# Row-wise exponentials on ScalarE in place of a subtraction and a row sum on VectorE, in linear attention with two MoE layers behind it

## The chip, the cores and the metric

The kernel runs on one core of a Trainium2 chip. The metric is the time of one execution on the device in microseconds, 1206.53 us as the median of three runs before the change. Five engines work side by side, each in its own program order: TensorE (PE for matmuls, PEld for weight loads), VectorE (DVE), ScalarE (ACT), GpSimd (POOL) and SyncE (SP, which issues the DMAs).

## The reference, cut to what matters

```python
# q, k, v: (8, 8, 576, 64)   batch, heads, tokens, head width
q_s = exp(q - max(q, -1));  q_s = q_s / (sum(q_s, -1) + 1e-9)   # along the 64 of a head
k_s = exp(k - max(k, 2));   k_s = k_s / (sum(k_s, 2) + 1e-9)    # along the tokens
out = q_s @ (k_s^T @ v)                                         # per head, 64 x 64 in between
x   = out as (4608, 512)
# first MoE layer: each token goes to argmax(x @ w_gate), one of 8 experts
x   = gate * sigmoid gate * (relu(x @ w1[e]) @ w2[e])
# second layer: the maximum of three products, then one more product
out = max(x @ W1, x @ W2, x @ W3) @ w_out
```

The change concerns only `q_s`: the maximum, the exponential and the sum over the 64 numbers of each head and token.

## The kernel before, in words

The kernel has two long parts. In the first, which lasts until about 600 us, attention and the first MoE layer are interleaved; the second MoE layer follows. The change touches the first part.

The first part is written as a list of slots. `moe_slot(slot)` issues one group of the MoE layer (`l1_group` or `l2_group`, 12 matmuls of 128 x 288 with a PSUM evacuation) and then the events that `at(slot, f, ...)` put into that slot. A batch has 32 slots: eight groups of the first product, eight of the second, for each of two halves of the hidden width. The schedule is manual: each engine runs its instructions in the order in which the slots issue them.

Attention comes in 16 units, one for each batch and half of the heads (`b, hb = divmod(n, 2)`), each spread over slots relative to its start `START[n] = 16 n - 51`, so a unit starts every 16 slots. `STEADY` gives the offsets of the first ten steps (`FRONT`): q_max -4, q_exp -1, k_max -4, k_tr 0, k_exp 1, q_sum 3, kv_mm 6, kv_norm 6, kv_lo 7, q_norm 8. Then come, for both pairs of heads (`BACK`), q_tr 10 and 15, q_lo 10 and 16, x_mm 13 and 17, x_lo 14 and 18, logit_mm 15 and 19. Units 0 to 3 have slots of their own. As a unit starts 16 slots after the one before it, slots -4 to 3 of a unit are slots 12 to 19 of the one before: the second half of its BACK steps and the FRONT steps of the next unit share slots. Events of the earlier unit come first in a slot.

A q tile has 128 partitions and 20 rows of 64 numbers (4 heads, 5 pieces of tokens). `q_max` (L230) takes the maximum of the 20 rows on VectorE. `q_exp` subtracts it (L237, VectorE; on GpSimd for one unit) and takes the exponential of all 1280 numbers in one ScalarE instruction (L238). `q_sum` sums the 20 rows on VectorE (L268), adds 1e-9 and takes the reciprocal (L269, L270). `q_norm` (L277) multiplies.

The other steps that the prediction names: `k_tr` transposes the key maxima (kT, L245), reduces them (L247) and forms the diagonal tiles dg with two products (L250); `k_exp` spreads them over the partitions with a matmul (kB, L257), subtracts on VectorE (L260) and takes the exponential on ScalarE (ke, L262). `q_tr` transposes q on TensorE and copies the upper part on ScalarE (qTs, L336), `q_lo` forms the lower part on VectorE (L344), and `x_mm` (xT, L362) multiplies with both, so it waits for q_lo. `logit_mm` (L390) copies the logits on ScalarE after the last pair (lgt, L393 and L394); one slot later `logit_tr` transposes them on TensorE (lg, L399), `route_1` follows on VectorE, and `route_2` counts with a matmul (cnt, L425).

Each MoE group is evacuated from one of four PSUM banks (`ps_mm`, bufs=4): in `l1_group` by a relu on ScalarE (L625) and a difference on VectorE (L626); in `l2_group` by a copy on ScalarE (L643) for the first half of the hidden width, and by an addition on VectorE (L645) for the second. The even units' slots -2 to 2 fall on groups with the ScalarE copy, those of the odd units on groups with the VectorE addition. Expert weights are split on ScalarE (L597) and GpSimd (L604), the weights of the second layer are decoded in three steps that share VectorE, ScalarE and GpSimd (L687 to L706), and the routing table is written by indirect DMAs from GpSimd (L498).

Of the kernel before, what the change touches and what calls it, by code (L numbers as in the profile page):

```python
# [9 lines left out]
F32 = mybir.dt.float32  # L10
# [3 lines left out]
ACTF = mybir.ActivationFunctionType  # L14
ALU = mybir.AluOpType
AX = mybir.AxisListType
# [37 lines left out]
ROUTE = (20, 22)  # L54
ROUTE0 = (7, 9)
ROUTE1 = (17, 19)
DEC = ((5, 10), (3, 8, 11), (18, 26))


@with_exitstack  # L60
def tile_linear_attention__then__moe(
# [18 lines left out]
    vec = nc.vector  # L80
    act = nc.scalar.activation
# [48 lines left out]
    sm = es_att.enter_context(tc.tile_pool(name="sm", bufs=2, side="right"))  # L130
# [52 lines left out]
    units = {}  # L183
# [35 lines left out]
    def k_max(b, hb):  # L219
        u = units[b, hb]  # L220
        u["mx"] = sm.tile([128, 4, D], F32, tag="kmx", name="kmx")
        vec.tensor_reduce(
            out=u["mx"], in_=u["k"].rearrange("p h c d -> p h d c"), axis=AX.X, op=ALU.max
        )

    def q_max(b, hb):
        u = units[b, hb]
        qt = u["q"].rearrange("p h c d -> p (h c) d")
        m = sm.tile([128, 20, 1], F32, tag="qm", name="qm")
        vec.tensor_reduce(out=m[:, :, 0], in_=qt, axis=AX.X, op=ALU.max)  # L230
        u["qm"] = m
# [274 lines left out]
    def at(slot, f, *args):  # L506
        events.setdefault(slot, []).append((f, args))
# [4 lines left out]
    def in_2(b, f):  # L512
        f(1, 0)

    first = (
        (load_k, 0), (load_k, 1), (load_q, 0), (load_v, 0), (load_q, 1), (load_v, 1),
        (k_max, 0), (k_tr, 0), (k_max, 1), (k_exp, 0), (k_tr, 1), (q_max, 0), (k_exp, 1), (q_exp, 0),
        (kv_mm, 0), (q_max, 1), (q_sum, 0), (kv_mm, 1), (q_norm, 0), (q_exp, 1), (kv_norm, 0), (q_tr, 0, 0), (kv_lo, 0),
        (load_2,), (q_sum, 1), (q_lo, 0, 0), (q_tr, 0, 1), (x_mm, 0, 0), (kv_norm, 1), (q_lo, 0, 1), (kv_lo, 1),
        (q_norm, 1), (q_tr, 1, 0), (x_mm, 0, 1), (logit_mm, 0, 0), (q_tr, 1, 1), (x_mm, 1, 0), (logit_mm, 0, 1),  # L520
        (x_mm, 1, 1), (x_lo, 0, 0), (x_lo, 0, 1), (logit_mm, 1, 0), (logit_mm, 1, 1), (in_2, q_max), (in_2, k_max),
        (logit_tr,), (route_1,), (route_2,), (in_2, q_exp), (x_lo, 1, 0), (x_lo, 1, 1), (route_3,),
    )
# [3 lines left out]
    for c in range(5):  # L527
        at(ROUTE0[1] + 2 * c, route_5, 0, c)
    START = {n: 16 * n - 51 for n in range(2, 2 * B)}
    FRONT = (q_max, q_exp, k_max, k_tr, k_exp, q_sum, kv_mm, kv_norm, kv_lo, q_norm)  # L530
    BACK = (q_tr, q_lo, x_mm, x_lo, logit_mm)
    for n, s0 in START.items():
        b, hb = divmod(n, 2)
        if n in EARLY:
            t, s0 = EARLY[n], 0
        else:
            t = STEADY
        if n > 2:
            at(LOAD.get(n, START.get(n - 2, 0) + 9), load_unit, b, hb)
        for d, f in zip(t[0], FRONT):  # L540
            if d is not None:
                at(s0 + d, f, b, hb)
        for pr in range(2):
            for d, f in zip(t[1 + pr], BACK):
                at(s0 + d, f, b, hb, pr)
        if hb == 1:
            s0 = START[n]
            r1, r2 = (s0 + ROUTE[0], s0 + ROUTE[1]) if n > 3 else ROUTE1
            at(r1, logit_tr, b)
            at(r1, route_1, b)  # L550
            at(r2, route_2, b)
            at(r2 + 3, route_3, b)
            at(r2 + 4, route_4, b)
            for c in range(5):
                at(r2 + 5 + 2 * c, route_5, b, c)
# [151 lines left out]

    dslots = [START[n] + o for n in range(4, 2 * B) for o in DEC[n % 2]] + [START[2 * B - 1] + o for o in DEC[2]]
    assert len(dslots) == 32
# [169 lines left out]
    with tc.manual_schedule():  # L879
# [458 lines left out]
        for c in range(6):  # L1338
# [41 lines left out]
            for i, (col, x) in enumerate(tiles):  # L1380
                m = CAP if x is None else 128
# [20 lines left out]
    with tc.For_i(0, n_trip, 1) as it:  # L1402
# [32 lines left out]
        for f in range(6):  # L1435
# [15 lines left out]
            h = lp.tile([128, 2, SLOT], F32R, tag=f"lh{f}", name="lh")  # L1451
# [44 lines left out]
```

## Time and profile before

| | |
|---|---|
| median of 3 runs | 1206.53 us (1205.19 to 1210.18) |
| profiled execution | 1209.64 us, its span 1207.9 us |
| PE busy | 1146.5 us, 95% of the span |
| DVE busy | 799.1 us, 66% |
| ACT busy | 527.4 us, 44% |
| POOL busy | 411.2 us, 34% |
| mean granted TensorE clock | 0.98 |

The page shows one execution. Busy time says how long an engine worked, not whether anybody waited for it; the waits and the timelines say that. A timeline row has the start, the duration (of all instructions that it merges), the engine, the line, the operation, the tiles written and read, the shapes and the count, and in brackets the idle time before it with what ended it.

### The profile page before, as it was taken

The page shows a single profiled execution, that of the slowest core. Times are in us where ns is not written, and L with a number is a line of the kernel's source. Part 1 is how long each engine was busy: PE and PEld are TensorE (multiplying, and loading weights), DVE is VectorE, ACT ScalarE, POOL GpSimd, SP SyncE. Part 2 cuts the span into 40 slices and gives each one's busy share as a digit, 9 for nine tenths or more (in the row PEclk, how much of TensorE's full clock was granted, in tenths as well). Part 3 has the DMA queues.
Part 4 walks back from the last instruction along what each step waited for, and adds up shares of the span by engine and source line. Part 5 has one row for each costly group of instructions (what it writes and reads, how often), then busy time and mean ns, then how long its engine had stood idle before and what let it go on. Part 6 is the DMA issues. An engine that isn't in the chain of part 4 may idle for free. (4 is left out here: it accounts for less than half of the span.)

```text
span 1207.9 us, 21422 instructions
## 1 busy us (share of the span) xinstructions
PE 1146.5 (95%) x7626; PEld 1072.1 (89%) x7626; DVE 799.1 (66%) x1500; ACT 527.4 (44%) x1081; POOL 411.2 (34%) x502
## 2 busy tenths in 40 slices
PE   4699999999989999999999999999999999999994
PEld 3599898989989898999999899899899989989983
DVE  7688788787878879655789565555546545564430
ACT  2454454635545453545455433443344244333220
POOL 1156667677666767768342030000000000000000
PEclk9899899999999999999999999999999999999997
DMA  6785557575645764436599588397768848747701
GB/s 162 181 224 135 160 170 218 153 208 156 180 159 170 203 177 137 137 115 204 195 311 311 176 256 285 134 296 242 235 217 272 270 144 286 242 149 221 225 26 41
DMA packets 204207, 234.95 MB, mean 195 GB/s; under 512 B 78253, under 2 KB 122061, under 8 KB 204096
## 3 DMA queue, kind: packets, MB, share of 16 engines
q1 hardware_dynamic: 202384, 233.14, 62.4%
q8 instruction: 62, 1.02, 0.3%
q0 software_dynamic: 1712, 0.39, 0.2%
q14 instruction: 49, 0.40, 0.1%
HBM read 189.56 MB, written 44.13 MB: 193 GB/s over the span
## 5 line engine op out<-in xcount | busy, mean ns | idle before, releaser
L638 PE MATMUL yp<-h,w 128*128 128x288 f32 x1536 | 227.0, 304 | 0.0
L620 PE MATMUL hp<-xs,w 128*128 128x288 f32 x1536 | 218.6, 299 | 0.0
L638 PEld LDWEIGHTS yp<-h,w 128*128 128x128 f32 x1536 | 213.1, 192 | 3.3
L620 PEld LDWEIGHTS hp<-xs,w 128*128 128x128 f32 x1536 | 208.2, 189 | 2.6
L604 POOL TENSOR_TENSOR w<-stg,w 128x512 fp32r<-128x512 f32 x126 | 181.2, 1441 | 68.5 <-ACT w L597 66.7
L1218 PE MATMUL pY<-t,sw 128*128 128x384 f32 (+1 forms) x972 | 193.5, 342 | 1.3 <-ACT s L1227 0.9
L1218 PEld LDWEIGHTS pY<-t,sw 128*128 128x128 f32 x972 | 172.8, 188 | 5.5 <-ACT s L1227 2.1
L1195 POOL DMA_INDIRECT out_dram<-ocx,ftb x1 | 1.0, 981 | 481.7 <-SPq L1402 481.7
L1306 PE MATMUL op<-wo,hc 128*128 128x512 f32 (+1 forms) x666 | 156.2, 394 | 0.0
L1306 PEld LDWEIGHTS op<-wo,hc 128*128 128x128 f32 (+1 forms) x666 | 125.1, 188 | 27.9
L1227 ACT ACTIVATE s<-pY 128x384 f32<-128x384 f32 (+1 forms) x108 | 53.7, 497 | 133.1 <-PE pY L1218 129.2
L626 DVE SCALAR_TENSOR_TENSOR h<-hp,h 128x288 fp32r<-128x288 f32 x128 | 56.6, 451 | 54.8 <-ACT h L625 54.4
L625 ACT ACTIVATE h<-hp 128x288 fp32r<-128x288 f32 x128 | 52.3, 409 | 83.1 <-PE hp L620 82.6
L597 ACT ACTIVATE w<-stg 128x512 fp32r<-128x512 f32 x128 | 78.9, 620 | 0.0
L1218 PE MATMUL pY<-B,sw 128*128 128x384 f32 (+1 forms) x324 | 66.4, 340 | 0.5 <-DVE y L645 0.5
L1218 PE MATMUL pZ<-B,sw 128*128 128x384 f32 (+1 forms) x324 | 66.8, 341 | 0.1
L1218 PE MATMUL pX<-B,sw 128*128 128x384 f32 (+1 forms) x324 | 66.9, 341 | 0.0
L1218 PE MATMUL pX<-t,sw 128*128 128x384 f32 (+1 forms) x324 | 66.5, 340 | 0.0
L1234 ACT ACTIVATE hc<-c 128x384 fp32r<-128x384 f32 (+1 forms) x72 | 38.2, 531 | 61.4 <-DVE c L1257 61.1
L1218 PEld LDWEIGHTS pZ<-B,sw 128*128 128x128 f32 x324 | 58.0, 188 | 2.2 <-DVE c L1251 0.4
L1218 PEld LDWEIGHTS pX<-B,sw 128*128 128x128 f32 x324 | 57.7, 188 | 1.7
L1218 PEld LDWEIGHTS pY<-B,sw 128*128 128x128 f32 x324 | 57.7, 188 | 1.7 <-DVE y L645 0.8
(246 smaller groups left out, 1764.0 us busy)
## 6 DMA issues: line engine op xcount, KB each, us to landing
sw<-ws_d SPq DMA_DIRECT2D x315, 256.0 KB, 3.5
stg<-in_moe_w_dram SPq DMA_DIRECT2D x31, 1024.0 KB, 5.3
ws_d<-sw SPq DMA_DIRECT2D x63, 256.0 KB, 3.4
fw<-in_moe_w_dram SPq DMA_DIRECT2D x48, 256.0 KB, 4.1
v<-in_v_dram SPq DMA_DIRECT2D x80, 128.0 KB, 4.7
draw<-in_moe_w_dram SPq DMA_DIRECT2D x24, 384.0 KB, 4.0
k<-in_k_dram SPq DMA_DIRECT2D x16, 512.0 KB, 5.3
q<-in_q_dram SPq DMA_DIRECT2D x16, 512.0 KB, 6.9
```

The costliest lines, as they stand in the source:

```text
L597: act(out=t[:, 0], in_=src, func=ACTF.Copy)
L604: eng.tensor_tensor(out=t[:, 1], in0=src, in1=t[:, 0].bitcast(F32), op=ALU.subtract)
L620: mm(ps, w[:, a, kk], xp[b, kk][:, c, cs], start=(n == 0), stop=(n == 11))
L625: act(out=h[:, 0, cs], in_=ps, func=ACTF.Relu)
L626: vec.scalar_tensor_tensor(out=h[:, 1, cs], in0=ps, scalar=0.0, in1=h[:, 0, cs].bitcast(F32), op0=ALU.max, op1=ALU.subtract,)
L638: mm(ps, w[:, a, f], ht[f][:, c, cs], start=(n == 0), stop=(n == 11))
L1195: nc.gpsimd.indirect_dma_start(out=out[:, :], out_offset=bass.IndirectOffsetOnAxis(ap=tb[0:n, 0:1], axis=0), in_=src, in_offset=None, boun ...
L1218: mm(ps[:, 0:nn], w[:, a, kap], tt_[key, kap][:, cc, 0:nn], start=(start and k == 0), stop=(k == 5), skip_group_check=True)
L1227: act(out=t[:, 0:n_of(c)], in_=pst[n, "X" if nm == "sx" else "Y"][:, 0:n_of(c)], func=ACTF.Copy)
L1234: act(out=h[:, 0, cols], in_=t[:, 0:nn], func=ACTF.Copy)
L1306: mm(ps[0:m], hc[f][:, a, col:col + m], wo[f][:, cc], start=(f == F_ORDER[0] and i == 0), stop=(f == F_ORDER[5] and i == 2))
```

## The change

From unit 4 on, `q_neg` takes the negated maximum in the place of `q_max`, and the events `q_exp` and `q_sum` are left out. In their place `q_rows` issues one ScalarE instruction per row: the exponential of 64 numbers with the negated maximum as a bias, one number for each partition, and with the sum of the row written to `qs` (`accum_out`). The 20 rows are spread over seven slots: 4 in slot -2, 2 in -1, 4 in 0, 3 in 2, 3 in 3, 2 in 4 and 2 in 5. `q_inv` adds 1e-9 and takes the reciprocal in slot 6; it was done in slot 3. `q_norm` stays in slot 8.

```diff
+QROWS = (((-2, 4), (-1, 2), (0, 4), (2, 3), (3, 3), (4, 2), (5, 2)), 6)
...
+    def q_neg(b, hb):
+        u = units[b, hb]
+        qt = u["q"].rearrange("p h c d -> p (h c) d")
+        m = u["qm"] = sm.tile([128, 20, 1], F32, tag="qm", name="qm")
+        vec.tensor_reduce(out=m[:, :, 0], in_=qt, axis=AX.X, op=ALU.max, negate=True)
+        u["qs"] = sm.tile([128, 20, 1], F32, tag="qs", name="qs")
+
+    def q_rows(b, hb, i0, i1):
+        u = units[b, hb]
+        qt = u["q"].rearrange("p h c d -> p (h c) d")
+        for i in range(i0, i1):
+            act(out=qt[:, i], in_=qt[:, i], func=ACTF.Exp, bias=u["qm"][:, i], accum_out=u["qs"][:, i])
+
+    def q_inv(b, hb):
+        s = units[b, hb]["qs"]
+        vec.tensor_scalar(out=s, in0=s, scalar1=1e-9, scalar2=None, op0=ALU.add)
+        vec.reciprocal(out=s, in_=s)
...
         for d, f in zip(t[0], FRONT):
-            if d is not None:
-                at(s0 + d, f, b, hb)
+            if d is None:
+                continue
+            if n >= 4 and f in (q_exp, q_sum):
+                continue
+            at(s0 + d, q_neg if n >= 4 and f is q_max else f, b, hb)
+        if n >= 4:
+            i0 = 0
+            for d, k_ in QROWS[0]:
+                at(s0 + d, q_rows, b, hb, i0, i0 + k_)
+                i0 += k_
+            at(s0 + QROWS[1], q_inv, b, hb)
```

## Rows read from the trace of the kernel before

**Rows 1.** The page, part 1: busy time, share of the span and instructions by engine.
```profile
PE 1146.5 (95%) x7626; PEld 1072.1 (89%) x7626; DVE 799.1 (66%) x1500; ACT 527.4 (44%) x1081; POOL 411.2 (34%) x502
```

**Rows 2.** Waits of TensorE: total us, how often, the longest.
```profile
PE xT L362 <- DVE qTs L344: 14.3, 6, 2.6
PE kB L257 <- DVE dg L250: 12.8, 6, 8.0
```

**Rows 3.** Timeline of TensorE, 112 to 142 us, the start of unit 5.
```profile
121.91 1.82 PE L638 MATMUL yp<-h,w 128*128 128x288 f32 x12
126.38 1.81 PE L362 MATMUL xT<-qTs,kvs 128*128 128x288 f32 x6 [2.64 <-DVE qTs L344]
```

**Rows 4.** Timeline of VectorE in the same stretch.
```profile
120.98 4.31 DVE L237 TENSOR_TENSOR q<-q,qm 128x1280 f32<-128x1280 f32 x1
125.21 0.45 DVE L645 TENSOR_TENSOR y<-yp,y 128x288 f32<-128x288 f32 x1
125.58 0.74 DVE L344 TENSOR_TENSOR qTs<-qT,qTs 128x576 fp32r<-128x576 f32 x1
```

**Rows 5.** Timeline of GpSimd in the same stretch.
```profile
122.91 1.02 POOL L705 TENSOR_TENSOR dr<-da,dr 128x384 f32<-128x384 f32 x1
124.76 1.43 POOL L498 DMA_INDIRECT tab_d<-tsrc,rpi  x1 [0.83 <-DMA tab_d<-tsrc,rpi]
```

**Rows 6.** Windows, kT to the second logits, odd units 5 to 15: the first, and all six.
```profile
121.77:133.84 12.07, 9.43 (x49) 8.79 (x47) 8.96 (x10) 4.92 (x6) 8.87 (x8) 0.72 0.53 171
...
sum 67.21, PE 50.44 PEld 46.38 DVE 54.58 ACT 29.50 POOL 45.11; mean PE 8.41 PEld 7.73 DVE 9.10 ACT 4.92 POOL 7.52
```
The columns are the length and the busy time (with instructions) of PE, PEld, DVE, ACT and POOL, then the granted clock, the DMA share and GB/s.

**Rows 7.** Windows, the same work in the even units 6 to 14: the first, and all five.
```profile
160.09:166.38 6.29, 6.29 (x48) 6.08 (x47) 4.14 (x7) 5.17 (x8) 2.94 (x2) 1.00 0.64 239
...
sum 31.44, PE 31.44 PEld 30.38 DVE 20.83 ACT 25.89 POOL 14.87; mean PE 6.29 PEld 6.08 DVE 4.17 ACT 5.18 POOL 2.97
```

**Rows 8.** Groups by line, whole span: count, busy us, mean ns, idle before.
```profile
L237 DVE TENSOR_TENSOR q<-q,qm 128x1280 f32<-128x1280 f32 x15 | 43.5, 2903 | 0.0
L268 DVE TENSOR_REDUCE qs<-q 128x20 f32<-128x1280 f32 x16 | 23.6, 1477 | 0.0
L238 ACT ACTIVATE q<-q 128x1280 f32<-128x1280 f32 x16 | 20.4, 1272 | 40.4 <-DVE q L237 37.7 <-POOL q L237 2.5
```

**Rows 9.** Groups by line, ScalarE instructions that bound the price of a row.
```profile
L1329 ACT ACTIVATE oc<-op,tsrc 128x512 f32<-128x512 f32 x32 | 22.0, 689 | 59.1 <-PE op L1306 45.7 <-issue 13.4
L1129 ACT ACTIVATE fraw<-fm 128x512 f32<-128x512 f32 x9 | 5.4, 598 | 4.7 <-PE fm L1108 4.7
L451 ACT ACTIVATE rex<-rd 128x40 f32<-128x40 f32 x8 | 1.8, 226 | 0.0
L457 ACT ACTIVATE rez<-rzs 128x5 f32<-128x5 f32 x8 | 1.7, 208 | 13.5 <-DVE rzs L455 13.5
```

**Rows 10.** Timeline of ScalarE, 112 to 142 us, the start of unit 5.
```profile
125.32 1.27 ACT L238 ACTIVATE q<-q 128x1280 f32<-128x1280 f32 x1 [4.50 <-DVE q L237]
```

**Rows 11.** Timeline of ScalarE, 150 to 172 us, the start of unit 6.
```profile
156.11 0.39 ACT L643 ACTIVATE y<-yp 128x288 f32<-128x288 f32 x1
...
166.53 0.39 ACT L643 ACTIVATE y<-yp 128x288 f32<-128x288 f32 x1
166.82 0.40 ACT L625 ACTIVATE h<-hp 128x288 fp32r<-128x288 f32 x1
...
167.27 0.20 ACT L394 ACTIVATE lgt<-lgT 32x64 f32<-32x64 f32 x1
```

**Rows 12.** Timeline of TensorE in that stretch of unit 6.
```profile
168.53 0.33 PE L399 MATMUL lg<-ident,lgt 128*128 128x64 f32 x2
```

**Rows 13.** Lines L344 and L250: duration of one in ns, least, median, greatest.
```profile
L344 DVE TENSOR_TENSOR qTs<-qT,qTs x24: 740/757/759, 112.1 to 512.4; 128x576 fp32r<-128x576 f32 x24
...
L250 DVE TENSOR_SCALAR dg<-ident,m x32: 274/284/1829, 9.1 to 482.1; 128x128 f32<-128x128 f32 x32
```

**Rows 14.** Window of unit 6, from slot -2 to the routing's one-hot; columns as in rows 6.
```profile
153.87:171.10 17.23, 17.23 (x142) 16.43 (x141) 13.94 (x21) 11.38 (x25) 11.04 (x8) 1.00 0.57 159
```

## The prediction

> **What bounds the kernel now.** I read first the shares of the engines, then the waits of TensorE, then the timelines around those waits. TensorE matmul is busy for 95% of the span [rows 1], so a change to VectorE and ScalarE can only pay where TensorE stands still or runs slowly. The list of its waits has one large entry in the steady part: x_mm's matmuls (xT, L362) wait for q_lo (L344) on VectorE, 14.3 us in 6 waits. The other large one, kB behind dg with 12.8 us in 6, has 8.0 us of it in a single wait in the opening stretch before unit 4, which the change does not touch [rows 2].
>
> The six waits are one pattern, once in each odd unit from 5 to 15. TensorE ends its group of 12 at 121.91 + 1.82 = 123.73 and starts x_mm at 126.38, 2.64 us late [rows 3]. VectorE is busy all that time: q_exp's subtraction of the next unit starts at 120.98 and lasts 4.31 us; q_lo stands behind it in VectorE's order and starts at 125.58 [rows 4]. The 4.31 us are mostly not VectorE's own work: GpSimd's product of the decoder (L705) runs from 122.91 to 123.93, its next instruction starts at 124.76 [rows 5], and the subtraction ends about 1.36 us after 123.93, about the time that a pass over 1280 elements takes undisturbed (the row sum's pass, 1477 ns [rows 8]). So it stood still beside GpSimd.
>
> What one such place costs is more than the wait, because the granted clock falls after it. From the k transposes to the logits of the second head pair TensorE has the same work in every steady unit. In the odd units these six stretches take 67.21 us, with PE busy 50.44 and the clock at 0.72 in the first of them [rows 6]; 0.72 is a mixture of the two levels, 2.4 and 1.2 GHz. In the even units five such stretches take 31.44 us, 6.29 each, all of it PE busy and at full clock [rows 7]. Six at 6.29 would be 37.7. So 67.2 - 37.7 = 29.5 us lie in these six places: 16.8 of waiting (67.21 - 50.44) and 12.7 of matmuls at the lower clock, 4.9 us a place.
>
> **The change part by part.** Twelve units (4 to 15) are changed.
>
> VectorE loses 12 subtractions and 12 row sums. The row sum is 1477 ns: 17.7 us. The subtraction averages 2903 ns over 15: about 35 us [rows 8]. The maximum becomes a negated maximum, the same pass, and q_inv keeps the two small operations of q_sum. So about 53 us leave VectorE. Nothing of that is a gain by itself, since VectorE is not the bound; what counts is that the 4.31 us go from in front of q_lo.
>
> What is late next in an odd unit: the y addition of that slot needs the group that ends near 121.9, and takes 0.45 us, so q_lo can run from about 122.4, ready at 123.1 with its 0.74 us [rows 4]. TensorE wants it at 123.73. Margin 0.6 us, so this wait goes. Then kB wants dg after x_mm, at about 124.6. Between q_lo and dg stand a reduction of about 0.4 us and two products, which end at about 124.1 at their fastest (274 ns each) and reach 1.8 us when one is held up [rows 13]. GpSimd has a pause from 123.93 to 124.76 [rows 5], just where they fall. I put 0.2 us a unit on it, 1.2 us in all; the ends are 0 and 1.4 us a unit (second rival).
>
> ScalarE loses one exponential of 1272 ns a unit [rows 8] and gains 20 small ones of 64 elements, each with a bias read from SBUF and a sum written out. The trace has no such instruction. From the rows: an exponential over 40 elements is 226 ns, and over 1280 it is 1272 [rows 8, 9], so 0.84 ns an element and 246 ns for 64. An evacuation of 512 columns with a scale read from SBUF is 689 ns and one without 598 [rows 9], so a pointer operand adds 91: 337 ns. Neighbours overlap by about 0.10 us (one of 0.39 us is followed after 0.29 us [rows 11]), so they follow each other at about 0.245 us. Writing out the sum is not in the trace: nothing at least, and at most one more smallest instruction without overlap (208 ns [rows 9]). So a row costs 0.245 us at the least and 0.337 + 0.208 = 0.55 at the most. I take 0.36, the pace plus a smallest instruction that overlaps like the others (0.208 - 0.09 = 0.12), since ScalarE's neighbours do overlap in the rows. Twenty rows are 7.2 us in place of 1.2: 6 us more a unit, 72 us in all, for an engine that is idle more than half of the span [rows 1].
>
> Where it lies matters more than the sum. In an odd unit ScalarE stood idle for 4.50 us, waiting for the subtraction [rows 10]; the ten rows of slots -2, -1 and 0 (3.6 us) fall there and in front of it, and nothing of TensorE waits. In an even unit I followed ScalarE's order by hand. Four rows after the y copy at 156.11 end at about 157.9, before anything is due. After the k exponential the y copy of 166.53 starts as before; then three new rows (1.1 us) stand between it and the relu of 166.82 [rows 11]. The relu moves to 167.9 and the last logit copy, which ended at 167.47, to 168.55. TensorE's logit transpose starts at 168.53 [rows 12]. So the margin of 1.06 us is just used up: I put 0.2 us a unit, 1.2 us in all. At 0.25 a row nothing waits; at 0.55 the earlier rows are late as well and it is about 0.9 us. The new wait is q_inv in slot 6, on the last two rows in slot 5, with the h differences queued behind it; at 0.36 these rows are done before the relu of slot 6, so nothing is added.
>
> The first rows wait for q_neg, which runs two slots earlier at the place of q_max. GpSimd shares its stretches with one pass less of VectorE, but TensorE does not wait for GpSimd [rows 2], so I count that at nothing. No DMA is added or moved; the first matmuls and the part after the attention are unchanged, and from there TensorE is the bound, so what is won before is kept.
>
> Sum against the profiled execution: 1209.64 - 29.5 + 1.2 + 1.2 = 1182.5. The median of the runs is 3.1 us below that execution, so 1179.4: I say **1180 us**.
>
> **A rule on the held-up products.** The rows show q_lo at 740 to 759 ns in all 24 cases and dg between 274 and 1829 [rows 13]. The Trainium skill (GPSIMD Engine Reference, 1. Specifications) says that GpSimd shares its SBUF interfaces with VectorE, and that the contention is with VectorE instructions that have two SBUF inputs or run in a two-port mode. By that rule the subtraction (two SBUF inputs) is exposed, q_lo (one input in PSUM) is not, as the trace agrees; and dg, with one SBUF input, can inherit the wait. This is the second rival.
>
> **The rivals.** First, ScalarE is late for the logits. If a row costs 0.55, the logit transpose waits 0.9 us and the count matmul behind the routing about 0.5, in six even units: 8 us, so 1187. If the clock falls after each too (12.7 / 6 = 2.1 us), 1200. For it: the margin is only 1.06 us. Against: rows at 0.39 us or less leave it whole.
>
> Second, dg takes the place of q_lo: GpSimd holds the products in each odd unit. The longest held product (1.83 us) in place of 0.27 gives a wait of about 1.4 us, six times 8.4: 1188; with the clock falling as now, 12.7 more: 1200. For it: the spread of dg. Against: GpSimd's pause just there.
>
> Third, the other side: ScalarE itself becomes the bound and holds PSUM. In the even stretch of 17.23 us ScalarE has 11.38 of work [rows 14], 10.1 without the old exponential, and gets 18 of the 20 rows. The group matmuls have four PSUM banks, so TensorE can be about three groups of 1.75 us ahead (1.82 with the tail of the last matmul [rows 3]), less 0.9 for the two evacuating instructions (0.40 and 0.45 [rows 4, 11]): 4.3 us. It stalls once 10.1 + 18 r - 17.23 is over 4.3, from r = 0.63 us a row. At 0.8 the stall is 3.0 us, with the clock 5.1, and the odd units lose some 4: 55 us lost against 29.5 won, 1232. It decides from about r = 0.75, twice my value and above the upper bound; only a sum that is waited for at each row gives that.
>
> Fourth, the waits go but the clock does not come back: only the 16.8 us, 1190. Against: the even units run at 1.00 with the same work. And last, something else than the subtraction keeps q_lo back and nothing changes: 1206. Against: rows 4 show nothing else on VectorE.
>
> **How the numbers follow.** Forecast 0.66 (own range 1174 to 1186), first rival 0.09, second 0.09, fourth 0.03, no change 0.05, third 0.08. What a measurement of this kernel can tell from no change is about 0.5%, 6 us. All of the forecast and the first, second and fourth rivals lie below 1200.5: faster 0.87, same 0.05, slower 0.08. Range 1173 to 1200: the lower end is the whole 29.5 us and 4 us of spread, the upper end takes in the first two rivals with the clock.
>
> **What would show it.** In the profile after: the wait of xT for q_lo gone from TensorE's list, its odd stretches near 6.3 us at clock 1.00; the row instructions 0.34 us long and 0.25 to 0.55 apart; ScalarE's busy time up by some 50 to 90 us and VectorE's down by about 53; new short waits, if any, of lg for lgt or kB for dg. TensorE waits on ScalarE's relu for PSUM, or stretches above 10 us, would make it wrong.

## The result and the profile after

The changed kernel takes 1197.51 us, median of five runs (1196.63 to 1199.51), against 1209.48 us (1205.19 to 1211.75) for the kernel before: a ratio of 0.9902 [0.9886, 0.9919], 12.0 us less. The forecast was 1180. The profiled execution after took 1197.52 us, its span 1195.5 us, 12.4 less than the span before.

The busy time of the engines, from the page of the changed kernel (beside [rows 1]):

```profile
PE 1136.8 (95%) x7626; PEld 1061.4 (89%) x7626; DVE 786.4 (66%) x1476; ACT 583.8 (49%) x1549; POOL 412.9 (35%) x502
```

VectorE has lost 12.7 us and not 53; ScalarE has gained 56.4.

TensorE's waits in the steady part (60 to 515 us) of the changed kernel; total us, how often, the longest:

```profile
PE yp L668 <- DVE h L656: 7.4, 6, 1.6
PE qT L350 <- DVE qn L298: 1.8, 2, 1.0
```

The wait of xT for q_lo [rows 2] is gone. In its place `yp`, the first group of the second MoE product, waits for the difference `h`, six times, once in each odd unit.

Two sets of windows tell how much went and came. First the six odd stretches from the k transposes to the second logits, after (columns as in [rows 6]):

```profile
122.09:128.46 6.37, 6.37 (x49) 6.11 (x47) 5.19 (x9) 4.45 (x13) 4.48 (x4) 1.00 0.74 218
...
sum 38.18, PE 38.18 PEld 36.66 DVE 31.15 ACT 26.69 POOL 26.79; mean PE 6.36 PEld 6.11 DVE 5.19 ACT 4.45 POOL 4.47
```

They were 67.21 us: 29.03 us are won, and the clock is 1.00, the 2.4 GHz level. Then the five stretches between them, from the second logits of an odd unit to the k transposes of the next odd unit, before:

```profile
133.84:193.45 59.61, 59.61 (x519) 57.01 (x519) 48.61 (x94) 31.14 (x67) 40.97 (x51) 1.00 0.62 178
...
sum 298.09, PE 298.09 PEld 285.07 DVE 243.46 ACT 155.26 POOL 209.23; mean PE 59.62 PEld 57.01 DVE 48.69 ACT 31.05 POOL 41.85
```

and after:

```profile
128.46:190.68 62.22, 60.43 (x519) 57.10 (x519) 51.82 (x90) 41.09 (x140) 45.08 (x54) 1.00 0.61 181
...
sum 310.83, PE 302.67 PEld 285.55 DVE 254.71 ACT 205.00 POOL 224.95; mean PE 60.53 PEld 57.11 DVE 50.94 ACT 41.00 POOL 44.99
```

They hold the same 519 matmuls each and are 12.74 us longer: 8.16 of it TensorE idle (310.83 - 302.67), the rest in rows that count as busy (302.67 against 298.09). VectorE is busy 11.3 us longer there, with 90 instructions in the first of them where it had 94. So 29.03 won, 12.74 given back between, 0.32 before the first place and 1.30 after the last: the last logit transposes come 14.67 us earlier (506.46 us into the span against 521.13). From the first matmul of the second layer to the end the profiled execution is 2.3 us longer (614.3 us against 612.0), which leaves the 12.4.

Where it is given back, in unit 5. TensorE:

```profile
142.83 1.59 PE L668 MATMUL yp<-h,w 128*128 128x288 f32 x10
145.99 3.18 PE L668 MATMUL yp<-h,w 128*128 128x288 f32 x22 [1.57 <-DVE h L656]
```

VectorE in front of that `h` (two differences, 145.49):

```profile
141.66 1.00 DVE L717 TENSOR_SCALAR df<-draw 128x384 int32<-128x384 int32 x1
142.70 1.53 DVE L719 SCALAR_TENSOR_TENSOR df<-draw,df 128x384 int32<-128x384 int32 x1
144.26 1.31 DVE L721 TENSOR_SCALAR dp<-df 128x384 int32<-128x384 int32 x1
145.49 0.81 DVE L656 SCALAR_TENSOR_TENSOR h<-hp,h 128x288 fp32r<-128x288 f32 x2
```

The same three decoder instructions before the change:

```profile
146.72 0.36 DVE L687 TENSOR_SCALAR df<-draw 128x384 int32<-128x384 int32 x1
147.11 0.56 DVE L689 SCALAR_TENSOR_TENSOR df<-draw,df 128x384 int32<-128x384 int32 x1
147.70 0.36 DVE L691 TENSOR_SCALAR dp<-df 128x384 int32<-128x384 int32 x1
```

1.28 us have become 3.84. And GpSimd beside them, after:

```profile
129.73 0.99 POOL L519 DMA_INDIRECT tab_d<-tsrc,rpi  x1 [2.42 <-DMA tab_d<-tsrc,rpi]
...
133.19 0.99 POOL L519 DMA_INDIRECT tab_d<-tsrc,rpi  x1 [1.14 <-DMA tab_d<-tsrc,rpi]
...
140.18 2.26 POOL L735 TENSOR_TENSOR dr<-da,dr 128x384 f32<-128x384 f32 x1
142.40 2.95 POOL L634 TENSOR_TENSOR w<-stg,w 128x512 fp32r<-128x512 f32 x2
```

and before:

```profile
129.64 0.99 POOL L498 DMA_INDIRECT tab_d<-tsrc,rpi  x1 [2.14 <-DMA tab_d<-tsrc,rpi]
...
141.39 1.01 POOL L705 TENSOR_TENSOR dr<-da,dr 128x384 f32<-128x384 f32 x1
...
148.19 1.01 POOL L695 TENSOR_TENSOR dr<-dr,dp 128x384 f32<-128x384 f32 x1 [2.91 <-ACT h L625]
```

This is the reading that the experiments had to test. GpSimd writes the routing table with five indirect DMAs in slots -5 to 3 of an odd unit. Two of these five wait for the one before, 2.42 and 1.14 us, with the products that split the expert weights queued behind. This chain hardly moved: the third write is issued at 129.64 before and at 129.73 after. TensorE, though, now has the matmuls of kv_mm (kv) at 133.87 instead of 139.26, having lost its stall. So the decoder product (L705, now L735) stood 2.1 us behind the kv matmuls and stands 6.3 us behind them now. Before, GpSimd caught up while TensorE stalled, and had 2.91 us of slack at 148.19. Now its late products run beside VectorE's decoder steps, which come out about three times as long and stand in front of `h`.

ScalarE is drawn in too. Its row of that moment:

```profile
142.47 0.56 ACT L722 ACTIVATE da<-draw 128x384 f32<-128x384 f32 x1 [2.94 <-POOL dr L735]
143.38 0.39 ACT L655 ACTIVATE h<-hp 128x288 fp32r<-128x288 f32 x1
```

It waits 2.94 us for the product to free the tile `da`, with a relu queued behind.

### The profile page after: what moved, and what is told of

Read it like the earlier page. It is cut to its first block, busy times and chain, and to the rows that moved or that the text cites. A ratio compares the mean times of both kernels' runs of the same rounds, so it can differ in the third digit from the quotient of the medians.

```text
span 1195.5 us, 21865 instructions
## 1 busy us (share of the span) xinstructions
PE 1136.8 (95%) x7626; PEld 1061.4 (89%) x7626; DVE 786.4 (66%) x1476; ACT 583.8 (49%) x1549; POOL 412.9 (35%) x502
## 5 line engine op out<-in xcount | busy, mean ns | idle before, releaser
L668 PE MATMUL yp<-h,w 128*128 128x288 f32 x1536 | 222.7, 299 | 7.4 <-DVE h L656 7.4
L668 PEld LDWEIGHTS yp<-h,w 128*128 128x128 f32 x1536 | 207.7, 188 | 11.4 <-DVE h L656 8.8
L240 ACT ACTIVATE q<-q,qm 128x64 f32<-128x64 f32 x240 | 80.1, 337 | 0.0
L1257 ACT ACTIVATE sx<-pX 128x384 f32<-128x384 f32 (+1 forms) x54 | 26.9, 497 | 67.6 <-PE pX L1248 64.2
```

What stands on the lines that cost most here:

```text
L240: act(out=qt[:, i], in_=qt[:, i], func=ACTF.Exp, bias=u["qm"][:, i], accum_out=u["qs"][:, i])
L668: mm(ps, w[:, a, f], ht[f][:, c, cs], start=(n == 0), stop=(n == 11))
L1257: act(out=t[:, 0:n_of(c)], in_=pst[n, "X" if nm == "sx" else "Y"][:, 0:n_of(c)], func=ACTF.Copy)
```

## The experiments

The theory: GpSimd, late against the slots, holds up VectorE (and ScalarE at `da`) in front of `h`. The rival: ScalarE's twenty rows make the relus late, and `h` with them. The experiments ran in five groups, each beside the kernel before, whose median there was 1208.32 to 1210.96 us. "Earlier" below is by how much the last logit transposes come before the 521.13 us of the kernel before; it leaves the second layer out.

**Odd units alone.**

```diff
-            if n >= 4 and f in (q_exp, q_sum):
+            if n >= 4 and hb == 1 and f in (q_exp, q_sum):
```

(and the same condition at q_neg and q_rows.)

> The change in the odd units 5 to 15 alone; the even units keep the subtraction, one exponential and the row sum on VectorE. The traces give 29.0 us won at the six odd places, 10.1 us lost about ten slots behind them and 4.7 us lost in the even units. If these even losses come from the even units' own rows and their moved VectorE work, this kernel gets the 4.7 us back: about 1193 us where the changed kernel is at 1197.5 and the kernel before at 1209.5. If they are GpSimd's lateness carried over from the odd units, it stays at 1197.

1199.37 us, 0.9918 [0.9902, 0.9935]: not told apart from the full change. Its waits of TensorE, 60 to 515:

```profile
PE kB L278 <- DVE dg L271: 6.0, 4, 1.5
PE yp L668 <- DVE h L656: 5.3, 6, 1.5
```

The win comes from the odd units. The 4.7 us of the even units don't come back: with their old subtraction they now lose at dg, whose two products take 2.41 us beside GpSimd's splits at 157.13 us.

**No subtraction, no rows.**

```diff
-            if n >= 4 and f in (q_exp, q_sum):
+            if n >= 4 and f is q_max:
                 continue
-            at(s0 + d, q_neg if n >= 4 and f is q_max else f, b, hb)
+            at(s0 + d, q_exp0 if n >= 4 and f is q_exp else f, b, hb)
```

The lines that issue `q_rows` and `q_inv` go as well. `q_exp0` is one exponential of 1280 numbers; the row sum stays on VectorE, and q's maximum is left out.

> From unit 4 on no maximum is taken and subtracted (left out: q's maximum, which cancels in the quotient); one exponential of 1280 numbers on ScalarE and the row sum on VectorE, as before. So the subtraction is gone from in front of q_lo and ScalarE gets no rows. Theory G (GpSimd, which no longer catches up while TensorE waits, holds VectorE's instructions in front of the last h differences): the six waits of the second product for h stay at 1.3 to 1.6 us, the time is 1194 to 1198. Rival S (the 20 rows make ScalarE's relus late): the six waits go, 1187 or less.

1192.87 us, 0.9872 [0.9855, 0.9889]. Its waits and its five stretches between:

```profile
PE qT L354 <- DVE qn L302: 5.0, 5, 1.4
PE yp L666 <- DVE h L654: 3.0, 6, 1.4
```

```profile
sum 307.65, PE 301.09 PEld 285.38 DVE 255.31 ACT 159.33 POOL 226.83; mean PE 60.22 PEld 57.08 DVE 51.06 ACT 31.87 POOL 45.37
```

ScalarE is back at its old load (159.33 against 155.26) and 9.56 us of the 12.74 are still given back. The rival falls as the main cause; the rows are worth 3.2 us between and 4.6 us of the median. The theory's own forecast is met in part only: the waits for `h` fall from 7.4 to 3.0 us, q_norm takes their place with 5.0, and the time lies below its 1194 to 1198.

**Decoder two slots later in odd units.**

```diff
-DEC = ((5, 10), (3, 8, 11), (18, 26))
+DEC = ((5, 10), (3, 10, 13), (18, 26))
```

> The changed kernel with the decoder's second and third piece of an odd unit in slots 10 and 13 in place of 8 and 11, so behind the last h differences of the first product. Theory G: the held-up decoder instructions no longer stand in front of the h differences, the six waits for h go and the time is about 1188, if nothing else stands at the new places. Rival S: the waits for h stay, 1197.

1218.65 us, 1.0066 [1.0044, 1.0087]: slower than the kernel before.

```profile
PE xT L383 <- DVE qTs L365: 13.2, 5, 4.5
PE qT L350 <- DVE qn L298: 6.0, 6, 1.0
```

The waits for `h` are gone, so the decoder steps are what stood in front of it; but they now stand in front of q_lo, and the forecast of 1188 is missed by 30 us. Much of that is not GpSimd: at the new places VectorE itself waits for the DMA that brings the piece's raw weights (`draw`), 27.1 us in 12 waits from 60 to 515 us, where the changed kernel has 3.2 in 5. One of them, in front of a q_lo:

```profile
155.58 0.36 DVE L717 TENSOR_SCALAR df<-draw 128x384 int32<-128x384 int32 x1 [3.06 <-DMA draw<-in_moe_w_dram]
```

**Table writes three slots apart, not two.**

```diff
-                at(r2 + 5 + 2 * c, route_5, b, c)
+                at(r2 + 5 + (3 if b < 7 else 2) * c, route_5, b, c)
```

> The changed kernel with the five table-writing DMAs of GpSimd three slots apart in place of two (the last batch as it was). Theory G in its full form (each of these DMAs waits for the one before, 1 to 2.4 us, with weight splits queued behind it, and this is what makes GpSimd late): GpSimd keeps up, the waits for h shrink to under 0.5 us, 1188 to 1191. If GpSimd is late for another reason (its products alone): 1197.

1207.45 us, 0.9985 [0.9976, 0.9995]: the forecast of 1188 to 1191 is missed. The longer chain reaches deeper into the odd unit: `h` is no longer waited for, but q_norm is.

```profile
PE qT L350 <- DVE qn L298: 14.3, 7, 2.7
```

**No table writes.**

```diff
-                at(r2 + 5 + 2 * c, route_5, b, c)
+                if b == 7:
+                    at(r2 + 5 + 2 * c, route_5, b, c)
```

> The changed kernel without the five table-writing DMAs of each batch but the last (left out: most of the routing table). Theory G (GpSimd is late because these DMAs wait for each other in the slots where it used to catch up): with them gone GpSimd keeps pace, the waits for h, qn and dg go, and what was won at the six places stays: last logit transpose of the first part about 25 to 29 us earlier than before in place of 14.7, time 1182 to 1186. If GpSimd is late by its products alone, the waits stay and the time is above 1192.

This kernel leaves most of the routing table unwritten. 1187.45 us, 0.9807 [0.9790, 0.9823]. Waits, and the five stretches between:

```profile
PE kB L278 <- DVE dg L271: 6.3, 7, 1.0
PE qT L350 <- DVE qn L298: 1.0, 1, 1.0
```

```profile
sum 300.10, PE 299.69 PEld 285.25 DVE 220.99 ACT 207.65 POOL 196.75; mean PE 59.94 PEld 57.05 DVE 44.20 ACT 41.53 POOL 39.35
```

With the chain gone, VectorE's busy time in the span falls from 786.4 to 756.9 us with the same 1476 instructions, and 10.73 of the 12.74 us come back (310.83 - 300.10). VectorE's own work is untouched here, so this is the run that puts the loss down to GpSimd. Now GpSimd is on time, and its splits fall on dg in the odd units. VectorE and GpSimd there:

```profile
124.51 1.92 DVE L271 TENSOR_SCALAR dg<-ident,m 128x128 f32<-128x128 f32 x2
```

```profile
123.84 2.51 POOL L635 TENSOR_TENSOR w<-stg,w 128x512 fp32r<-128x512 f32 x2
```

That is the second rival of the prediction, 1 us a place; the odd stretches are 45.10 us in place of 38.18. So the last logit transposes come 19.05 us earlier, not the 25 to 29 of the forecast. Of the 8.6 us by which the profiled span is shorter than with the change, 4.4 lie before them and 4.2 in the second layer (610.1 us against 614.3), which is not explained.

**Four splits of each odd unit on VectorE**, in the change, without the subtraction, and in the kernel before:

```diff
-        eng = vec if s < 2 else nc.gpsimd
+        eng = vec if s < 2 or s in ON_VEC else nc.gpsimd
```

`ON_VEC` holds the splits of slots -4, 2, 4 and 6 of the odd units.

> The changed kernel with four weight splits of each odd unit (slots -4, 2, 4 and 6) on VectorE in place of GpSimd: GpSimd saves four times 1.3 us, VectorE takes four times 0.7 us. Theory G: GpSimd's lateness of about 6 us at the decoder of slot 8 shrinks to about 1, the waits for h fall below 0.4 us each, 1187 to 1190. Rival: VectorE's own length of work in front of the h differences is what counts; then the waits grow, above 1198.

> The same four splits on VectorE in the kernel without maximum, subtraction and rows (left out: q's maximum, which cancels in the quotient). There the waits for qn and h after the odd units cost about 11 us in all. Theory G: most of them go, 1182 to 1186 from 1192.9. Otherwise 1192 or more.

> The kernel before with the same four splits on VectorE, so the control. The subtraction still stands in front of q_lo, and the two GpSimd instructions that hold it are not moved: the six waits of 2.3 us and the lower clock behind them stay, 1205 to 1214. If moving splits were worth something by itself, it would be under 1203.

1206.23 (0.9967 [0.9955, 0.9978]), 1191.50 (0.9852 [0.9834, 0.9870]) and 1208.02 us (0.9990 [0.9979, 1.0002]). In the changed kernel the split of slot -4 stands in front of q_lo and brings that wait back, 1.0 us in each odd unit; the waits for `h` halve. Without the subtraction q_lo isn't held, yet nothing is won either: the five stretches between are 308.02 us against 307.65 in no_shift, the waits for `h` 3.7 us against 3.0. Both forecasts of the theory are missed: as a relief of GpSimd this doesn't pay, since VectorE takes the work. The waits of split_vec:

```profile
PE xT L383 <- DVE qTs L365: 6.2, 6, 1.0
PE yp L670 <- DVE h L658: 3.6, 5, 0.8
```

**Table writes moved into the even units**, alone, with dg on ScalarE in the odd units, the latter without the subtraction, and in the kernel before:

```diff
-                at(r2 + 5 + 2 * c, route_5, b, c)
+                at(r2 + (24 if b < 7 else 5) + 2 * c, route_5, b, c)
```

```diff
+            if b >= 2 and hb == 1:
+                act(out=u["dg"][:, i], in_=ident, func=ACTF.Copy, scale=m2[:, i:i + 1])
+                continue
```

> The changed kernel with the five table-writing DMAs of batches 1 to 6 moved 19 slots later, from slots -5 to 3 of an odd unit to slots -2 to 6 of the even unit behind it. Theory G: the odd units come out as in the kernel without these DMAs (no wait for h or qn, dg 1.0 us late), 1187 to 1191, if the even units bear them; if the even units' dg or qn is held in their place, 6 times 1 to 2 us are lost there and the time stays at 1195 to 1199.

> The same, with the two products of dg in the odd units from 5 on taken on ScalarE (a copy with a scale for each partition) in place of VectorE. Without the table writes dg was held 1.0 us behind GpSimd in the odd units. Theory G: that wait goes too, 6 to 9 us below the kernel with the moved writes alone. If dg is late for another reason (the reduction in front of it), no difference.

> Both moves in the kernel without maximum, subtraction and rows (left out: q's maximum, which cancels in the quotient; it stood at 1192.9). Theory G: its waits for qn and h go, 1180 to 1185, the whole of the 29 us won at the six places less about 3. If the rows on ScalarE were no part of the loss, the two kernels with both moves differ by the 4.6 us of before at most.

> The kernel before with the table writes moved alone, the control. The subtraction stays in front of q_lo. GpSimd's split and product that hold it come up to 1.4 us earlier without the table write at 120.2, so the six waits can shrink from 2.3 to about 1 us; the clock after them decides: 1195 to 1203. If the writes' place matters only once the subtraction is gone: 1206 to 1212.

1207.39 (0.9976 [0.9962, 0.9989]), 1199.37 (0.9913 [0.9893, 0.9933]), 1197.92 (0.9898 [0.9878, 0.9917]) and 1214.78 us (1.0037 [1.0023, 1.0052]). With the writes moved, the waits of scat_even are

```profile
PE kB L278 <- DVE dg L271: 6.1, 6, 1.0
PE qT L350 <- DVE qn L298: 3.6, 3, 1.3
PE cnt L446 <- ACT dr L724: 3.2, 3, 1.1
```

so the odd units look as they do with no writes (stretches of 45.20 us against 45.10), and the stretches between, which hold the even units, are 311.85 us: they pay instead, and both forecasts are missed. With dg on ScalarE its wait goes, and 8 us with it. In the kernel before the same move costs 5 us, with dg the new wait (10.8 us in 11). With dg moved the last logit transposes come 16.1 us earlier (against 14.67 with the change) and, without the subtraction, 19.8 (against 18.2 in no_shift), but the time is no better: from there to the second layer scat_even_dg takes 78.3 us where the changed kernel takes 74.8.

**A decoder piece of the odd units moved to the even ones**, in three kernels; in dec_b the second piece of the even units moves as well, from slot 10 to 8:

```diff
-DEC = ((5, 10), (3, 8, 11), (18, 26))
+DEC = ((5, 10, 13), (8, 11), (18, 26))      # dec_a, no_shift_dec_a, before_dec_a
+DEC = ((5, 8, 11), (8, 11), (18, 26))       # dec_b
```

> The changed kernel with one decoder piece moved from slot 3 of the odd units to slot 13 of the even units (three pieces in the even, two in the odd units); table writes as in the changed kernel. If GpSimd's amount of work in the odd units is what makes it late (theory G): some 3 us less in front of slot 8, the waits for h of 1.3 to 1.6 us go, 1187 to 1191. If the writes' waiting for each other alone makes it late: 1196 to 1199. If the piece at slot 13 (just in front of q_lo and dg of the odd unit) holds these: above 1200.

> The piece moved as in dec_a, in the kernel without maximum, subtraction and rows (left out: q's maximum, which cancels in the quotient; 1192.9 without the move). Theory G: its waits for qn and h, 1 to 1.4 us each in the odd units, go: 1182 to 1187. Otherwise 1192.

> The kernel before with the piece moved as in dec_a, the control: the subtraction is still held behind GpSimd, the six waits of xT stay, 1205 to 1214.

> The same with the even pieces in slots 5, 8 and 11. Theory G: slot 8 of the even unit lies in front of its last h differences, but GpSimd is on time there, so little is lost; the odd units' waits for h go: 1188 to 1192. Otherwise 1197 or more.

1225.25 (1.0134 [1.0112, 1.0156]), 1220.54 (1.0085 [1.0054, 1.0116]), 1231.72 (1.0206 [1.0164, 1.0248]) and 1235.56 us (1.0216 [1.0190, 1.0242]): all slower. In dec_a the waits for `h` are gone and the five stretches between are 300.08 us, as the theory has it; but the piece stands in front of q_lo, and the odd stretches are 78.81 us in place of 38.18:

```profile
PE xT L383 <- DVE qTs L365: 23.3, 6, 4.4
```

Slot 13 of an even unit is slot -3 of the odd one. VectorE there waits for the DMA of the piece's raw weights, and ScalarE for GpSimd at the one `da`:

```profile
122.51 1.64 DVE L717 TENSOR_SCALAR df<-draw 128x384 int32<-128x384 int32 x1 [2.61 <-DMA draw<-in_moe_w_dram]
123.95 0.55 ACT L722 ACTIVATE da<-draw 128x384 f32<-128x384 f32 x1 [5.96 <-POOL dr L735]
```

In dec_b it is the logits of the even units that wait (lgT behind ScalarE's copy `xr`, 20.8 us in 6), in before_dec_a xT again (30.7 in 6). The control is a miss too: 1205 to 1214 was forecast, so the place costs 22 us without the change as well. The misses show that a piece at these places is paid for at the next step that TensorE needs.

**One decoder piece less in each odd unit**, with the six pieces put into the last slots of unit 15.

```diff
-DEC = ((5, 10), (3, 8, 11), (18, 26))
+DEC = ((5, 10), (8, 11), (14, 17, 20, 23, 26, 29, 32, 34))
```

> The changed kernel with the six decoder pieces of slot 3 of the odd units taken behind the last units (slots 14 to 34 of unit 15, three apart), everything else as in the changed kernel. Theory G: the waits for h in the odd units (7.4 us in six) fall below 2 us in all, 1186 to 1190, less what the tail of the first part loses by its six more pieces. If GpSimd is late without that piece too: 1196 to 1199.

> The same in the kernel without maximum, subtraction and rows (left out: q's maximum, which cancels in the quotient; 1192.9 without the move). Theory G: 1180 to 1186. Otherwise 1192.

1207.98 (0.9981 [0.9970, 0.9993]) and 1203.54 us (0.9932 [0.9913, 0.9950]). The six odd stretches of dec_c:

```profile
sum 38.17, PE 38.17 PEld 36.67 DVE 31.86 ACT 26.71 POOL 27.31; mean PE 6.36 PEld 6.11 DVE 5.31 ACT 4.45 POOL 4.55
```

The five between, of dec_c and then of no_shift_dec_c:

```profile
sum 300.58, PE 299.92 PEld 285.25 DVE 219.09 ACT 202.14 POOL 201.49; mean PE 59.98 PEld 57.05 DVE 43.82 ACT 40.43 POOL 40.30
```

```profile
sum 298.20, PE 298.20 PEld 285.16 DVE 221.34 ACT 156.31 POOL 203.14; mean PE 59.64 PEld 57.03 DVE 44.27 ACT 31.26 POOL 40.63
```

Of the 12.74 us, 10.25 go with one decoder piece a unit (310.83 to 300.58), a further 2.38 with the rows (to 298.20), and what is left is 0.11: the stretches of the kernel before, with the 29 us of the odd places still won. The piece takes its own work off VectorE and ScalarE too, so dec_c alone does not tell GpSimd's hold from their own load; no_scatter does. The last logit transposes come 24.85 and 28.97 us earlier. The median doesn't show it (1186 to 1190 was forecast for dec_c, less what the tail loses), since the six pieces stand packed in the slots of unit 15 and are paid for there: from the last logit transposes to the second layer dec_c takes 94.4 us in place of 74.8. Two of its waits of TensorE, 490 to 600 us:

```profile
PE hp L650 <- DVE h L656: 6.0, 1, 6.0
PE yp L668 <- DVE y L675: 4.6, 1, 4.6
```

Of the versions that compute everything, the changed kernel stayed the best in the median (odd_only and scat_even_dg, both 1199.37, are not told apart from it); no_shift, no_shift_split and no_scatter, which leave something out, are below it. No place for the six pieces was found that costs nothing. A second `da` tile was not tried.

## Why the prediction was right in its direction and wrong in its size

- **The six odd places.** Forecast 29.5 us by 67.21 to 37.7; measured 29.03, with the wait gone and the clock at 1.00. The fourth rival (clock lost) and the last one (something else holds q_lo) fall. This term was right, and its reason: the variants without the long subtraction in front of q_lo have it, until a split or a decoder piece is put there instead or dg is held behind GpSimd.
- **The price of a row.** Forecast 0.36 us; the trace has an exponential of 337 ns, as worked out, and a read-out of the sum of 191 ns, and a pair follows the last after 0.33 us:

```profile
128.62 0.33 ACT L240 ACTIVATE q<-q,qm 128x64 f32<-128x64 f32 x1
128.85 0.19 ACT L240 ACTIVATION_READ_ACCUMULATOR q<-q,qm 128x1 f32 x1
128.95 0.33 ACT L240 ACTIVATE q<-q,qm 128x64 f32<-128x64 f32 x1
```

- **ScalarE in the even units.** Forecast 1.2 us over six; the difference of dec_c and no_shift_dec_c puts the rows at 2.38 over five stretches, odd and even units together. Twice the estimate, still small. The first rival at its size (8 us) and the third (ScalarE the bound) fall.
- **dg.** Forecast 1.2 us. In the odd stretches it cost at most 0.5 (38.18 against 37.7). It came to 1 us a place in no_scatter and scat_even, where the table writes are gone from the odd units: the second rival was there, hidden as long as GpSimd was late.
- **The step that failed** is "GpSimd shares its stretches with one pass less of VectorE, but TensorE does not wait for GpSimd [rows 2], so I count that at nothing". Between the odd places 12.74 us were lost, where the sum had only the 1.2 us of the even units; 10.73 of them come back when GpSimd's table writes alone are left out (no_scatter), 10.25 with one decoder piece a unit less (dec_c). TensorE doesn't wait for GpSimd in the list after either: GpSimd holds VectorE, and VectorE's `h` holds TensorE. The list of waits names the last link only. The stretch with the stall was also GpSimd's time to catch up, and GpSimd, with table writes that wait for one another, did not get faster when TensorE did. "So what is won before is kept" was said of the part behind the attention; there the profiled execution lost 2.3 us.
- **VectorE's 53 us.** The instructions are gone, but only 12.7 us of busy time, because others got longer beside GpSimd. The first step of the decoder grew most, before and then after:

```profile
L687 DVE TENSOR_SCALAR df<-draw 128x384 int32<-128x384 int32 x32 | 13.0, 405 | 7.6 <-DMA draw<-in_moe_w_dram 4.1 <-DMA draw<-in_moe_w_out_dram 2.3 <-POOL w L604 1.2
```

```profile
L717 DVE TENSOR_SCALAR df<-draw 128x384 int32<-128x384 int32 x32 | 26.8, 836 | 4.5 <-DMA draw<-in_moe_w_dram 2.3 <-DMA draw<-in_moe_w_out_dram 2.0
```

  The other decoder steps and q_norm (26.9 to 31.8 us over 16) add about 5 us each.
  The 4.31 us of the subtraction [rows 4] had shown such a hold; the prediction took it for a property of that instruction's place, and it moved to the next instructions that GpSimd met.
- **The sum.** 29.03 - 12.74 - 0.32 - 1.30 - 2.3 = 12.4 us. The 2.3 us in the second layer are seen (614.3 us against 612.0, and 610.1 to 614.6 in the other traces), not explained.
- **The range.** 1197.51 lies within the stated 1173 to 1200, but by luck: the upper end came from rivals that lose the clock after each wait, and the clock stayed at 1.00. The forecast also took 3.1 us off for a median below the profiled execution; with five runs that gap was 0.16 us (1209.64 against 1209.48).

## What to carry to other kernels

Removing a stall of the bounding engine also removes the time in which the other engines caught up. Before counting a won wait as kept, take the engines that are paced by something other than the bounding one (here a chain of DMAs on GpSimd), shift the bounding engine's times by the win, and read off how late they then are and which in-order queue, buffer or port they hold up. To see where such a gain goes, compare windows of equal work around and between the places; the shares of busy time and the list of waits show only its last link.

## What the runs showed of the hardware

- A sum written out by ScalarE's exponential is an instruction of its own, 191 ns, of which 0.09 us appear in the pace (0.33 us in place of the 0.24 that the overlap of neighbours gives). No trace of before had it.
- Short VectorE instructions beside GpSimd's products end close to the end of the product: the decoder steps on int32 go from 0.36 to 1.00 and 1.31 us and from 0.56 to 1.53, two dg products from 0.55 to 1.92. GpSimd pays as well: its product L735 took 2.26 us in place of 1.01. q_lo, with one operand in PSUM, kept its 0.74. The Trainium skill (GPSIMD Engine Reference, 1. Specifications) has the contention with VectorE instructions with two SBUF inputs or in a two-port mode; the traces agree for q_norm, L719 and q_lo. L717, L721 and dg have one input tile in SBUF, so by that rule they ran in such a mode, which no trace shows.
- The 1.57 us wait of TensorE in the changed kernel left the granted clock at 1.00 (the window 128.46 to 190.68 above, with 1.79 us idle), while the stretch with the 2.64 us wait before had 0.72 [rows 3, 6].
